# Sums of raw blocks of x by accumulating transfers instead of VectorE additions, in the weight gradient of a strided convolution

## The chip, the cores and the metric

The kernel runs on one core of a Trainium2 chip. TensorE multiplies matrices into PSUM, VectorE and ScalarE work element by element, and transfers run on 16 DMA engines that all queues share. A transfer is issued either by SP (SyncE) or by GpSimd (POOL in the profile); the profile shows the two as a hardware queue and a software queue. The metric is the time of one execution on the device in microseconds.

## The reference

A one-dimensional convolution with stride 2 (31 taps, 256 channels to 256), a normalization over time and a GELU, and then the gradients of all of it for a given `grad_out`:

```python
B, T, D, K = 2, 16000, 256, 31
s = 2
L = (T - K) // s + 1
h = jnp.einsum('blc,cd->bld', x[:, 0:s * L:s, :], w[0])
for i in range(1, K):
    h = h + jnp.einsum('blc,cd->bld', x[:, i:i + s * L:s, :], w[i])
mu = jnp.einsum('bld->bd', h)[:, None, :] / L
var = jnp.einsum('bld->bd', (h - mu) ** 2)[:, None, :] / L
h = (h - mu) / jnp.sqrt(var + 1e-5)
h = h * gn_gamma[None, None, :] + gn_beta[None, None, :]
return _gelu(h)
...
_out, _vjp = jax.vjp(_f, x, w, gn_gamma, gn_beta)
_grads = _vjp(grad_out)
```

The outputs are the forward result and the gradients for x, w, gamma and beta, in bfloat16. The change is in the gradient for w: for each tap i it is the sum over time of x at the tap's position times the gradient d of the convolution's output.

## The kernel before

The program has three large stages on TensorE: the forward convolution (with the GELU beside it), the gradient for x, and the gradient for w. The last one is the function `gradw` (line 1102) and the only one that the change touches.

**The algorithm of the stage.** The taps are split by the bits of their index, and each of three levels trades four products for three: two "corner" products, A and C, and a middle product B of the sum of two blocks of x with the difference of two blocks of d. Two levels give the nine combinations `COMBOS` (line 1100), n = 0 to 8; the third level is inside a combination. In combination n, x is needed as two tiles per half of the batch, `tgt[n, b, k3]` for k3 = 0 and 1, and as their sum `xs[n, b]`. A tile holds 128 partitions x 8 x 512 bf16 elements, 1 MB. Where neither outer level is a middle, a tile is one raw block of x, as `x_raws` lists it; with one middle it is the sum of two raw blocks, and in combination 3, which is (B, B), of four. These sums are the subject of the change.

**TensorE.** In each combination `leaf` runs 64 matmuls on the sums `xs` against d (two halves h, each over both b), then 64 on the tiles with k3 = 1 and 64 on those with k3 = 0, all 128x128 by 128x512. Four PSUM tiles hold the partial products; between them ScalarE copies and VectorE additions (`wps`, `p`, `we` in the profile) combine the three levels. `emit` makes a finished pair of taps in a tile `we`, of which there are two, and GpSimd stores it to `out_2`.

**VectorE.** Besides that it makes the differences of d (`d_sub` on the tiles D, E, S; `mk_dl` for the third level), the sums of raw blocks (`x_add`, 128x4096 elements) and the sums of the two tiles (`x_sum`).

**Transfers.** SP loads raw blocks with `raw` (line 1112: a tile's row is eight pieces of 1 KB from DRAM) and blocks of d with `d_raw` (the tiles D, E, S, 1216 KB). GpSimd stores `we`, and in the last two combinations also the late rows of `out_0`, which SP turns from `yd` into free x tiles (`out0_row`).

**Order.** It is written out by hand. Every engine works through its own queue in program order, and the program order follows a clock that counts TensorE's time: `advance(us)` moves it, `at(t, fn)` puts a step at a time, and `d_plan` and `x_plan` set the times of loads, additions and sums for combination n + 1 relative to the start T of combination n (a combination is some 41 us). So the times in the plans decide where an instruction stands in its engine's queue; when it then runs follows from the semaphores.

**Tiles.** `free` is a list of seven x tiles, and three more (`xe`) come from before the stage. A tile goes back with `release` when its matmuls are issued; the next write to it waits for TensorE to have read it: the tiles with k3 = 1 come free two thirds of the way through a combination, those with k3 = 0 at its end. Two fp32 tiles, `p2`, are lent to the list as `spare` in one combination. The tiles of combination 1, each a sum of two blocks, are kept as the first terms of combination 3 (`release` with n == 1).

**Before the change** `x_load(n, b, k3, j)` loads raw block j of a tile into a tile from `free`: j = 0 into the target itself, j > 0 into a temporary tile `tmp`. `x_add(n, b, k3, j)` with j > 0 adds the temporary tile to the target on VectorE and gives it back to `free`. With j = 0 it adds the tile of combination 0 to the raw block of combination 1, as (A, B) needs.

Of the kernel before, what the change touches and what calls it, by code (L numbers as in the profile page):

```python
# [12 lines left out]
ALU = mybir.AluOpType  # L13
# [17 lines left out]
def conv_stem_kernel(  # L31
# [14 lines left out]
    NB, T, C = x.shape  # L46
# [82 lines left out]
    te, ve, ac, gq, sp_ = (Engine(e) for e in (nc.tensor, nc.vector, nc.scalar, nc.gpsimd, nc.sync))  # L129
# [84 lines left out]
    def add2(out, a, b):  # L214
        return ve.tensor_tensor(out=out, in0=a, in1=b, op=ALU.add)
# [464 lines left out]
    def at(t, fn):  # L680
        clock[1] += 1
        events.append((t, clock[1], fn))
# [402 lines left out]
    def xblk(b):  # L1085
        t0 = 0 if b == 0 else NB * T - P * P
        return xf[t0:t0 + P * P, :].rearrange("(p f r par) c -> p f r (par c)", p=P, f=8, r=8, par=2)
# [14 lines left out]
    def gradw(px, po, psw, Dt, Et, St, x0):  # L1102
# [3 lines left out]
        xs_0 = [side["e"].tile([P, 2 * EH * 4], BF16, name="xh", tag="he", bufs=2)[:, 0:2048].rearrange("p (f n) -> p f n", f=4)  # L1106
                for _ in range(2)]
        free = [px.tile([P, 8, 512], BF16, name="x2", tag="x2", bufs=7)[:] for _ in range(7)]
# [3 lines left out]
        def raw(t, b, k3, k1, k2):  # L1112
            sp_.dma_start(out=t, in_=xblk(b)[:, :, 4 * k3 + 2 * k2 + k1, :])
            return t

        tgt, tmp = {}, {}

        def x_raws(n):
            i1, i2 = COMBOS[n]
            if (i1, i2) == (B_, B_):  # L1120
                return [None, (0, 1), (0, 0)]
            if (i1, i2) == (A, B_):
                return [(1, 0)]
            return [(k1, k2) for k1 in raws[i1] for k2 in raws[i2]]

        def x_load(n, b, k3, j=0):
            k = x_raws(n)[j]
            t = raw(free.pop(0), b, k3, *k)
            if j:
                tmp[n, b, k3, j] = t  # L1130
            else:
                tgt[n, b, k3] = t

        def x_add(n, b, k3, j):
            t = tgt[n, b, k3]
            if j:
                r = tmp.pop((n, b, k3, j))
                add2(t, t, r)
                free.append(r)
            else:  # L1140
                r = tgt[n - 1, b, k3]
                if r is xs_0:
                    for i in range(2):
                        add2(t[:, 4 * i:4 * i + 4], r[i], t[:, 4 * i:4 * i + 4])
                else:
                    add2(t, r, t)

        def x_sum(n, b):
            xs[n, b] = free.pop(0)
            if tgt[n, b, 0] is xs_0:  # L1150
                for i in range(2):
                    f = slice(4 * i, 4 * i + 4)
                    add2(xs[n, b][:, f], xs_0[i], tgt[n, b, 1][:, f])
            else:
                add2(xs[n, b], tgt[n, b, 0], tgt[n, b, 1])
# [49 lines left out]
        def x_plan(n, T):  # L1205
            def ld(t, n, b, k3, j=0):
                at(T + t, lambda: x_load(n, b, k3, j))

            def ad(t, n, b, k3, j):
                at(T + t, lambda: x_add(n, b, k3, j))  # L1210
            four = ((0, 1), (0, 0), (1, 1), (1, 0))
            if n == 1:
                for j, k in enumerate(four):
                    ld(1 + j, n, *k)
                    ad(18 + 4.2 * j, n, *k, 0)
            elif n in (2, 7, 8):
                for j, k in enumerate(four):
                    ld(1 + j, n, *k)
                if n == 2:
                    for j in (1, 2):  # L1220
                        ld(14 + j, 3, 0, 1, j)
                        ad(28 + j, 3, 0, 1, j)
            elif n == 3:
                for j, (t0, t1, b, k3, i) in enumerate(((14.5, 23, 0, 0, 1), (15, 25, 0, 0, 2), (15.5, 27.5, 1, 1, 1), (16, 29, 1, 1, 2),
                                                        (24, 34.5, 1, 0, 1), (26, 37, 1, 0, 2))):
                    ld(t0, n, b, k3, i)
                    ad(t1, n, b, k3, i)
            else:
                for k, t0, t1 in zip(four, (1, 3, 17.5, 20), (14.5, 17, 29.5, 32)):
                    ld(t0, n, *k)  # L1230
                    ld(t0 + 1, n, *k, 1)
                    ad(t1, n, *k, 1)
            for b in range(NB):
                at(T + ((36, 38.5) if n == 1 else (33.5, 38))[b], lambda b=b: x_sum(n, b))

# [95 lines left out]
        for n in range(9):  # L1331
            i1, i2 = COMBOS[n]
            T, d2, dl = clock[0], Et if i2 == B_ else Dt, {}
# [5 lines left out]
            if n == 7:  # L1339
                for i in range(8):  # L1340
                    t = T + (17 if i == 0 else 20.5 + 6 * i)
                    at(t, lambda i=i: out0_row(i, False))
                    at(t + 13, lambda i=i: out0_row(i, True))
            if n < 8:
                d_plan(n + 1, T)
                x_plan(n + 1, T)
# [17 lines left out]
            for i3, G in ((A, Y), (C_, X)):  # L1364
                k3 = 1 if i3 == A else 0
# [8 lines left out]
            if n == 2:  # L1374
# [10 lines left out]
                n=(14, 28, 42, 58, 82, 102, 150, 180, 228, 241, 262, 275, 298, 310, 332, 344),  # L1385
# [38 lines left out]
    def conv(b, c, ahead, prev):  # L1424
        nonlocal kn
        k, kn = kn, None

        def nxt():
            nonlocal kn
            if kn is None:  # L1430
                kn = FChunk(*ahead, xts.pop(ahead))
            return kn
        if ahead:
            at(clock[0] + 2, lambda: xts.__setitem__(ahead, fwd_load(*ahead)))
        return k, fwd_chunk_fixed(k, nxt if ahead else None, prev, advance)

    for c in range(1, NCK):
        k, prev = conv(0, c, (0, c + 1) if c + 1 < NCK else (1, 0), prev)
# [23 lines left out]
    for c in range(NCK):  # L1462
        k, prev = conv(1, c, (1, c + 1) if c + 1 < NCK else None, prev)
# [124 lines left out]
    for n, (b, c) in enumerate(seq):  # L1588
        k = kn
# [36 lines left out]
    with tc.tile_pool(name="px", bufs=1, reuse_waits="tile") as px, \  # L1626
            tc.tile_pool(name="psw", bufs=2, space=bass.MemoryType.PSUM, reuse_waits="tile") as psw:
        gradw(px, px, psw, Dt, Et, St[0], x0)
# [38 lines left out]
```

## Time and profile before

| | us |
|---|---|
| median of three runs (1272.4 to 1275.49) | 1272.7 |
| profiled execution | 1270.96 |
| span of its profile, first to last instruction | 1269.1 |
| first matmul of `gradw`, from the span's start | 893.0 |
| starts of combinations 1 to 8 | 935.3, 976.8, 1018.2, 1059.6, 1101.1, 1142.7, 1184.4, 1225.9 |
| VectorE addition of two 1 MB tiles | 2.28 |
| load of a block of x on SP's queue, median to landing | 8.6 |

The nine combinations can be told in the trace by the tiles that TensorE reads: `wps<-D,x` or `wps<-E,x` starts one, `wps<-dl,x` are its inner tiles. Nearly every instruction carries line 125, that of the recording helper, so groups are told apart by tile names. In the lines of the DMA queues q1 is SP's hardware queue and q0 GpSimd's software queue: packets, MB, and the time of their packets as a share of the 16 engines' span of the window. The DMA share in a window is the mean busy share of those engines. In the timeline, a bracket at the end of a line holds the idle time of the engine just before and what ended it.

### The profile page before, as it was taken

To read this page: it belongs to the slowest core of one execution; us is meant where nothing else is said; L and a number is where in the kernel's file an instruction comes from. 1 tells how busy PE (TensorE), PEld (TensorE's weight loads), DVE (VectorE), ACT (ScalarE), POOL (GpSimd) and SP (SyncE) were. 2 spreads that over 40 slices of the span, in tenths; PEclk is the share of its full clock that TensorE was granted. 3 is DMA by queue.
4 is the path that set the end of the run, shared out by engine and by line. 5 is a ranking of instruction groups with operands and counts; after the bars stand their busy time and mean duration, and the time that the engine had idled before them with its cause. 6 is when DMAs were issued, how large, how long until landed. Compare 5 with 4: busy or idle time off the path is not lost.

```text
span 1269.1 us, 19006 instructions
## 1 busy us (share of the span) xinstructions
PE 1233.0 (97%) x7692; PEld 758.6 (60%) x7692; DVE 901.7 (71%) x1080; ACT 504.0 (40%) x679; POOL 279.8 (22%) x410
## 2 busy tenths in 40 slices
PE   4899999999999999999999999999999999999998
PEld 2788889988888964444445444445444444444444
DVE  3967656578988687989876596685576755876482
ACT  0032423489888568989853333222011010101000
POOL 2013201112222433445333331100000000110043
PEclk9999999999999999999999999999999999999999
DMA  9979987439997796998649995455894795997895
GB/s 199 176 153 196 215 150 138 79 77 197 185 164 159 208 305 157 208 226 234 172 148 107 241 237 121 127 183 170 277 325 150 232 333 188 322 337 262 252 226 127
DMA packets 289335, 252.73 MB, mean 199 GB/s; under 512 B 197128, under 2 KB 260616, under 8 KB 284128
## 3 DMA queue, kind: packets, MB, share of 16 engines
q1 hardware_dynamic: 254448, 152.60, 50.7%
q0 software_dynamic: 30576, 96.82, 29.7%
q10 hardware_dynamic: 4224, 2.10, 0.8%
q8 instruction: 60, 0.98, 0.3%
q14 instruction: 27, 0.22, 0.1%
HBM read 136.42 MB, written 68.63 MB: 162 GB/s over the span
## 4 chain that ended last, share of the span: by engine, by line
PE 49%; DVE 3%; issue 2%; DMA 1%; ACT 1%; POOL 1%; POOLq 0%; DVEq 0%; ACTq 0%
PE wps L125 28%; PE ps L125 20%; DVE D L125 1%; DMA dyd<-gg 1%; DMA x<-in_x_dram 1%; DVE ps L125 0%; DVE et L125 0%; DVE le L125 0%; DVE go L125 0%; DVE ux L125 0%; POOL he L125 0%; DVE s L125 0%; DMA gg<-got 0%; DVE vk L125 0%; ACT gy L125 0%
## 5 line engine op out<-in xcount | busy, mean ns | idle before, releaser
L125 PEld LDWEIGHTS <-w 128*128 128x128 bf16 x3360 | 327.5, 98 | 57.7 <-issue 10.5
L125 PE MATMUL ps<-v,le 128*128 128x512 bf16 (+3 forms) x1152 | 259.2, 375 | 2.6 <-DVE ps L125 2.4
L125 PEld LDWEIGHTS <-le 128*128 128x128 bf16 (+1 forms) x1280 | 129.9, 102 | 144.8 <-issue 4.3
L125 PEld LDWEIGHTS <-x 128*128 128x128 bf16 x1248 | 122.0, 98 | 144.6 <-DVE x L125 0.6
L125 PE MATMUL ps<-la,w 128*128 128x256 bf16 (+2 forms) x1200 | 135.2, 273 | 18.0 <-DVE la L125 17.7
L125 PE MATMUL wps<-dl,x 128*128 128x512 bf16 (+1 forms) x704 | 150.8, 374 | 0.0
L125 ACT ACTIVATE ps<-ps 128x1024 f32<-128x1024 f32 (+3 forms) x115 | 85.2, 741 | 147.0 <-PE ps L125 147.0
L125 PE MATMUL ps<-lc,w 128*128 128x256 bf16 (+2 forms) x1168 | 129.2, 270 | 0.0
L125 ACT COPY p<-wps 128x1024 f32<-128x1024 f32 x28 | 28.4, 1013 | 211.2 <-PE wps L125 106.7
L125 DVE TENSOR_TENSOR go<-ps,rg 128x1024 bf16<-128x1024 f32 (+1 forms) x64 | 78.0, 1220 | 43.8 <-PE ps L125 29.1
L125 POOL DMA_DIRECT2D out_dram<-we x31 | 22.5, 726 | 334.6 <-DVE we L125 334.6
L125 PE MATMUL ps<-v,ux 128*128 128x512 bf16 (+1 forms) x384 | 90.7, 379 | 3.6 <-DVE ux L125 1.9
L125 PE MATMUL wps<-dl,xe 128*128 128x512 bf16 x416 | 91.7, 379 | 0.0
L125 PE MATMUL ps<-lx,w 128*128 128x256 bf16 (+2 forms) x768 | 86.9, 270 | 1.8 <-ACT ps L125 1.3
L125 ACT ACTIVATE gy<-gh,stats 128x1024 bf16<-128x1024 bf16 x64 | 76.6, 1228 | 7.3 <-DMA gh<-hd 7.3
L125 PE MATMUL wps<-D,x 128*128 128x512 bf16 x352 | 77.1, 379 | 0.0
L125 PEld LDWEIGHTS <-xe 128*128 128x128 bf16 x416 | 40.7, 98 | 49.1
L125 PEld LDWEIGHTS <-ux 128*128 128x128 bf16 (+1 forms) x384 | 38.7, 101 | 49.3 <-DVE ux L125 3.6
L125 ACT ACTIVATE hs<-ps 128x512 bf16<-128x512 f32 (+1 forms) x64 | 36.7, 578 | 75.9 <-PE ps L125 75.9
L125 DVE TENSOR_TENSOR ps<-ps,rb 128x1024 f32<-128x1024 f32 (+1 forms) x37 | 38.0, 1028 | 36.2 <-ACT rb L125 28.3
L125 ACT COPY rg<-ps 128x1024 f32<-128x1024 f32 (+1 forms) x32 | 32.2, 1007 | 69.2 <-PE ps L125 67.4
L125 DVE SCALAR_TENSOR_TENSOR gz<-gy,gy 128x1024 bf16<-128x1024 bf16 x32 | 39.1, 1222 | 23.9 <-ACT gy L125 22.8
(170 smaller groups left out, 1708.4 us busy)
## 6 DMA issues: line engine op xcount, KB each, us to landing
x<-in_x_dram SPq DMA_DIRECT2D x29, 1024.0 KB, 8.6
xe<-in_x_dram SPq DMA_DIRECT2D x20, 1024.0 KB, 9.2
S<-dnd SPq DMA_DIRECT2D x16, 1216.0 KB, 8.3
D<-dnd SPq DMA_DIRECT2D x12, 1216.0 KB, 9.2
out_dram<-go POOLq DMA_DIRECT2D x28, 512.0 KB, 4.2
gh<-hd POOLq DMA_DIRECT2D x32, 256.0 KB, 7.3
dnd<-dn POOLq DMA_DIRECT2D x32, 256.0 KB, 4.4
E<-dnd SPq DMA_DIRECT2D x6, 1216.0 KB, 10.6
```

Of the source, the lines that this page charges most:

```text
L125: ins = fn(*a, **k)
```

## The change

Where a tile is the sum of several raw blocks, the second and further blocks are no longer loaded into temporary tiles by SP and added by VectorE. Instead GpSimd issues a transfer with `accum_op=ALU.add` from x in DRAM into the target tile: the transfer adds the block to what the tile holds. This concerns 20 blocks: eight in combination 3 (two into each of its four tiles, on top of the tile kept from combination 1), and four each in combinations 4, 5 and 6. The temporary tiles are gone, and so the tiles go round in another order. The plan's times are new: in combinations 4 to 6 the plain loads stand at 1, 3, 13 and 15 us and the accumulating transfers at 9, 12, 22 and 25 (before: loads at 1, 2, 3, 4, 17.5, 18.5, 20 and 21, additions at 14.5, 17, 29.5 and 32); in combination 3's plan the six accumulating transfers stand at 2, 8, 12, 17, 21 and 26, and the two of its first tile at 29 and 37 in the combination before. An accumulating transfer waits for whatever wrote the tile before it. The function `add2` and all of the rest are unchanged.

```diff
         def x_load(n, b, k3, j=0):
-            k = x_raws(n)[j]
-            t = raw(free.pop(0), b, k3, *k)
+            k1, k2 = x_raws(n)[j]
             if j:
-                tmp[n, b, k3, j] = t
+                gq.dma_start(out=tgt[n, b, k3], in_=xblk(b)[:, :, 4 * k3 + 2 * k2 + k1, :], accum_op=ALU.add)
             else:
-                tgt[n, b, k3] = t
-
-        def x_add(n, b, k3, j):
-            t = tgt[n, b, k3]
-            if j:
-                r = tmp.pop((n, b, k3, j))
-                add2(t, t, r)
-                free.append(r)
+                tgt[n, b, k3] = raw(free.pop(0), b, k3, k1, k2)
+
+        def x_add(n, b, k3):
+            t, r = tgt[n, b, k3], tgt[n - 1, b, k3]
+            if r is xs_0:
+                for i in range(2):
+                    add2(t[:, 4 * i:4 * i + 4], r[i], t[:, 4 * i:4 * i + 4])
             else:
...
+                add2(t, r, t)
...
                 if n == 2:
                     for j in (1, 2):
-                        ld(14 + j, 3, 0, 1, j)
-                        ad(28 + j, 3, 0, 1, j)
+                        ld(21 + 8 * j, 3, 0, 1, j)
             elif n == 3:
-                for j, (t0, t1, b, k3, i) in enumerate(((14.5, 23, 0, 0, 1), (15, 25, 0, 0, 2), (15.5, 27.5, 1, 1, 1), (16, 29, 1, 1, 2),
-                                                        (24, 34.5, 1, 0, 1), (26, 37, 1, 0, 2))):
-                    ld(t0, n, b, k3, i)
-                    ad(t1, n, b, k3, i)
+                for t, b, k3, i in ((2, 0, 0, 1), (8, 1, 1, 1), (12, 0, 0, 2), (17, 1, 0, 1), (21, 1, 1, 2), (26, 1, 0, 2)):
+                    ld(t, n, b, k3, i)
             else:
-                for k, t0, t1 in zip(four, (1, 3, 17.5, 20), (14.5, 17, 29.5, 32)):
+                for k, t0, t1 in zip(four, (1, 3, 13, 15), (9, 12, 22, 25)):
                     ld(t0, n, *k)
-                    ld(t0 + 1, n, *k, 1)
-                    ad(t1, n, *k, 1)
+                    ld(t1, n, *k, 1)
```

More of the change, by code (lines that the diff above doesn't have):

```diff
@@ L1114, in raw @@
             return t
-        tgt, tmp = {}, {}
+        tgt = {}
         def x_raws(n):
@@ L1126, in x_load @@
         def x_load(n, b, k3, j=0):
-            k = x_raws(n)[j]
-            t = raw(free.pop(0), b, k3, *k)
+            k1, k2 = x_raws(n)[j]
             if j:
-                tmp[n, b, k3, j] = t
+                gq.dma_start(out=tgt[n, b, k3], in_=xblk(b)[:, :, 4 * k3 + 2 * k2 + k1, :], accum_op=ALU.add)
             else:
-                tgt[n, b, k3] = t
-        def x_add(n, b, k3, j):
-            t = tgt[n, b, k3]
-            if j:
-                r = tmp.pop((n, b, k3, j))
-                add2(t, t, r)
-                free.append(r)
-            else:
[L1141 to L1146, printed above, removed]
+                tgt[n, b, k3] = raw(free.pop(0), b, k3, k1, k2)
[4 more added lines that the diff above has]
+                    add2(t[:, 4 * i:4 * i + 4], r[i], t[:, 4 * i:4 * i + 4])
+            else:
+                add2(t, r, t)
         def x_sum(n, b):
@@ L1207, in ld, with ad @@
                 at(T + t, lambda: x_load(n, b, k3, j))
-            def ad(t, n, b, k3, j):
-                at(T + t, lambda: x_add(n, b, k3, j))
+            def ad(t, n, b, k3):
+                at(T + t, lambda: x_add(n, b, k3))
             four = ((0, 1), (0, 0), (1, 1), (1, 0))
@@ L1214, in x_plan @@
                     ld(1 + j, n, *k)
-                    ad(18 + 4.2 * j, n, *k, 0)
+                    ad(18 + 4.2 * j, n, *k)
             elif n in (2, 7, 8):
```

## The prediction

> **What bounds the kernel now.** I read the busy shares first, then the windows cut at the nine combinations of the weight gradient (the only code that the change touches), then the chain that ended last, and at the end the DMA queues in those windows, because the change turns VectorE work into transfers. From the page:
>
> ```profile
> PE 1233.0 (97%) x7692; PEld 758.6 (60%) x7692; DVE 901.7 (71%) x1080; ACT 504.0 (40%) x679; POOL 279.8 (22%) x410
> ```
>
> The windows of combinations 2 to 6 (us; then busy us of PE, PEld, DVE, ACT, POOL with counts; granted clock, DMA share, GB/s):
>
> ```profile
> 976.80:1018.20 41.40, 41.40 (x194) 18.74 (x192) 31.62 (x20) 4.06 (x4) 0.00 (x0) 1.00 0.62 189
> 1018.20:1059.60 41.40, 41.40 (x193) 18.81 (x192) 24.00 (x12) 6.05 (x6) 0.00 (x0) 1.00 0.88 289
> 1059.60:1101.10 41.50, 41.50 (x194) 18.80 (x193) 29.23 (x17) 4.05 (x4) 4.40 (x6) 1.00 0.82 268
> 1101.10:1142.70 41.60, 41.60 (x194) 18.80 (x193) 29.43 (x20) 4.05 (x4) 5.18 (x8) 1.00 0.97 339
> 1142.70:1184.40 41.70, 41.55 (x192) 18.69 (x192) 27.58 (x15) 6.05 (x6) 2.06 (x3) 1.00 0.81 278
> ```
>
> TensorE fills every combination: 192 matmuls of 0.216 us are 41.4 us, which is the window. VectorE is busy for 24 to 32 us of it, so taking VectorE work away frees nothing. The DMA engines are the second resource, at 0.97 in combination 5. The chain shows that this is already the tight place:
>
> ```profile
> 1099.95 39.30 PE wps L125 x182
> 1139.24 0.02 issue
> 1139.26 7.14 DMA x<-in_x_dram
> 1146.40 0.02 issue
> 1146.42 53.70 PE wps L125 x248
> ```
>
> Between 1139 and 1146 the chain runs through a load of x, and the timeline shows what that costs TensorE (idle 0.26 and 0.64 us):
>
> ```profile
> 1142.66 3.12 PEld L125 LDWEIGHTS <-x 128*128 128x128 bf16 x15 [0.26 <-issue]
> 1146.41 3.57 PEld L125 LDWEIGHTS <-x 128*128 128x128 bf16 x18 [0.64 <-DVE x L125]
> ```
>
> These 0.9 us are the whole idle time of TensorE in the stage, and so the most the change can win.
>
> **The change part by part.** *Removed from VectorE:* 20 additions of 128x4096 at 2.28 us, 45.6 us. Cover: TensorE's 41.4 us per combination. Worth 0, at most the 0.9 us above.
>
> *Removed from SP:* the 20 loads of 1 MB that fed them. What stays on SP moves up past them, but most of it waits for TensorE to release a tile (SP waited 110 us in the stage for that), so it starts little earlier. Worth 0.
>
> *Issue on GpSimd:* 20 issues. A store of hs has as many pieces (1024) and took 0.89 to 0.92 us, so 18 us over four combinations on an engine busy for 5 us of 41 there. Worth 0.
>
> *New waits on GpSimd's queue:* an accumulating transfer waits until the plain load of its tile has landed, and the second one into a tile of combination 3 waits for the first. Behind it in the queue stand the stores of we (combinations 4 and 5); two we tiles rotate, so a late store holds VectorE's next we addition, and that holds the PSUM tile that TensorE needs. In combinations 2 and 3 nothing stands behind. I cost it at nothing by itself: two of a combination's four accumulations stand ahead of its first store, and the other two wait for loads that have landed some 17 to 28 us into it (three blocks and two D in a row are 16.4 us of the engines, more with accumulations between), while the second group of stores leaves 29 us into combination 4 today (1089.0).
>
> *The last stores of out_0:* the tiles that the late transposes take change. Two of the four are now free only when combination 8 starts (1225.9), where today their transposes start at 1221.6. Their stores leave at 1256.6, 13 us after the last transpose was issued, so a shift of 4 us is hidden.
>
> *The transfers themselves* decide. The trace has no accumulating transfer; its nearest rows on the page (KB each, median us from issue to landing) are
>
> ```profile
> x<-in_x_dram SPq DMA_DIRECT2D x29, 1024.0 KB, 8.6
> ...
> out_dram<-go POOLq DMA_DIRECT2D x28, 512.0 KB, 4.2
> ```
>
> Call a the time that one 1 MB block takes of all 16 DMA engines. A plain load of a block, from combination 2, where the queue moved almost nothing else:
>
> ```profile
> q1 hardware_dynamic: 7720, 7.79, 61.6%
> ```
>
> 61.6% of 41.4 us is 25.5 us for 7.79 MB, so 3.43 us a block (1.05 MB). Lower bound: a = 3.43, if reading the old content of the tile hides behind the read of x. A read of SBUF is priced by the stores of we in combination 5:
>
> ```profile
> q0 software_dynamic: 384, 1.05, 6.5%
> ```
>
> 1.05 MB cost 6.5% of 41.6 us, 2.70 us. If an engine does both reads one after the other, a = 3.43 + 2.70 = 6.13. Upper bound, nothing overlapped: the landing time of a load (8.6 us) and of two 512 KB stores (4.2 each), a = 17. I take 6.13: it lies nearest to the rows that count engine time and not latency, and many pieces are in flight in every transfer here. A rule speaks against the change at this very place. The Trainium skill, Collectives: The Full Stack, section "The bandwidth ceiling: the fold count and why AG ≠ RS ≠ AR", says that a reducing transfer puts two reads per piece on one read ring, and gives 62.28 against 32.35 GB/s, a ratio of 1.93. By it a would be 6.6 (an estimate: 1.93 times 3.43) and the end some 9 us later than mine; no run here shows it.
>
> Now the demand on the DMA engines by combination, with 3.43 for a block of x, 3.07 for a load of D, E or S (combination 1: 30.7 us for 11.24 MB, of which 3.77 MB of x took 12.3; six loads remain), 2.7 for eight stores of we:
> - combination 2: 6 accumulations, half of one left over from combination 1, 2 loads of E: 6.1 + 6.5a
> - combination 3: 4 blocks, 2 D, 4 accumulations: 19.9 + 4a
> - combination 4: the same and the stores: 22.6 + 4a
> - combination 5: 4 blocks, 4 loads of E and S, stores, 4 accumulations: 28.7 + 4a
>
> Together 77.3 + 18.5a against 4 x 41.4 = 165.8 us of TensorE. At a = 3.43 combination 5 needs 42.4, which is what it does today (8 loads instead of 4 and 4). At a = 6.13 the four need 45.9, 44.4, 47.1 and 53.2, together 190.7: 24.9 us too much. No combination shows a share over 0.97, so 190.7 becomes 196.6: 5.9 more. At three of the ends (of 2, 4 and 5) TensorE then stands until the last accumulation has landed and VectorE has made the sum: 2.3 (shortest landing 5.7 less 3.43) + 2.28, less the 3.45 us of 16 matmuls that run before the second half's sum is needed, 1.1 each, 3.3 in all. At the last of them a load of the next combination stands in the other queue and takes 3.4 of the engines' time. Sum: 24.9 + 5.9 + 3.3 + 3.4 - 0.9 (today's idle time) = +36.6 us. The profiled execution took 1270.96 us (span 1269.1), so 1307.6; the median of the runs shown is 1.7 above it: 1309 us.
>
> **The rivals.** *The second read is hidden (not slower).* For it: reads and writes of an engine may overlap, and in combinations 2 and 3 the share is 0.62 and 0.88, so there is room. Against: in combination 5 there is none. It decides at one point: with a up to 4.4, combination 5 needs 46.3, 4 us more than today, combination 4 40.2, and the end moves by less than 0.3% (about what a measurement of this kernel can tell from no change). Time 1271.8 (a = 3.43 and no idle time) to 1276.5. A gain over 0.3% would need 3.8 us of idle time where the trace has 0.9; I leave it a rest for what I have overlooked in the stage before.
>
> *The pieces are handled one after another (much slower).* If an engine waits for one sum before the next read, a goes by latency; the nearest row is a load's landing, 8.6 us. Then 77.3 + 159.1 = 236.4, 70.6 too much, 7.3 for the share, 6.7 for the ends, -0.9: +83.7, so 1356 and more. Against it: a load of 1 MB lands after 8.6 us though each engine has 64 pieces of it, so pieces of plain transfers do overlap.
>
> *The stores behind the accumulations become the wait.* If a plain load lands late, GpSimd's queue stands and with it the stores of we. VectorE's third we addition of combinations 4 and 5 would then be late by up to one accumulation, some 6 us: 12 us on top of the forecast, 1321. It needs the transfers to be late first, so it is a part of the slower cases.
>
> That the change does not do what it says is excluded: the program as built has 20 additions fewer on VectorE, 20 loads fewer on SP and 20 transfers more on GpSimd.
>
> **How the numbers follow.** Forecast, a from 4.4 to 8.6: chance 0.52 (with the stores' rival 0.07 of it), own range 1277 to 1356, likeliest 1309. Hidden: 0.26, of which 0.03 for faster by over 0.3% and 0.23 within it. One after another: 0.22. So faster 0.03, within 0.3% 0.23, slower 0.74. The range goes from 1268, which takes in the hidden case, to 1362, which takes in the beginning of the last one; some 0.18 lies above.
>
> **What would show it.** Right: accumulating transfers with a DMA share near 1 in combinations 2 to 5, TensorE idle at the starts of combinations 3, 5 and 6 behind an addition of x (the sum) that waits for a transfer of GpSimd's queue, combinations 0, 1, 7 and 8 unchanged at 41.4. GpSimd's queue time for 20 MB of accumulations gives a directly: 123 us of 16 engines at 6.13. Wrong: a DMA share in combination 5 that stays at 0.97 with TensorE full (hidden), or landings of tens of us while the share is low (latency, not engine time). A loss outside combinations 2 to 6 would mean that I have missed a place.

## The result and the profile after

| | before | after |
|---|---|---|
| median, us | 1272.88 (1272.4 to 1275.49) | 1296.99 (1295.31 to 1297.97) |
| profiled execution, us | 1270.96 | 1297.31 |
| stage: first matmul of `gradw` to the start of combination 8, us | 893.01 to 1225.86: 332.85 | 894.11 to 1252.25: 358.14 |

The change makes the kernel slower: ratio 1.0183, 95% interval 1.0167 to 1.0199, some 24.1 us. The forecast was 1309, 36.6 us more than before. The stage alone grew by 25.3 us; combinations 0, 1, 7 and 8 did not grow. Further down I compare stages too, because the time at which the stage begins differs by some us from one profiled execution to the next (889 to 906 in the runs of this study), although everything ahead of it is the same program.

The line of busy times of the page of after, and its software queue, which now carries the 20 blocks:

```profile
PE 1236.8 (95%) x7692; PEld 759.3 (59%) x7692; DVE 857.1 (66%) x1060; ACT 503.8 (39%) x679; POOL 309.6 (24%) x430
...
q0 software_dynamic: 51376, 117.80, 39.3%
```

VectorE has lost its 20 additions (901.7 to 857.1 us, 1080 to 1060 instructions), GpSimd has 20 instructions more and is busy for 29.8 us more. TensorE has the same 7692 matmuls but is busy for 3.8 us more: some matmuls run slower.

The windows of combinations 2 to 6 of after (us; busy us of PE, PEld, DVE, ACT, POOL with counts; granted clock, DMA share, GB/s):

```profile
977.90:1019.30 41.40, 41.40 (x194) 18.77 (x193) 13.30 (x10) 4.05 (x4) 7.29 (x6) 1.00 1.19 207
1019.30:1062.70 43.40, 41.57 (x193) 18.67 (x192) 14.86 (x8) 6.04 (x6) 6.08 (x5) 1.00 1.13 267
1062.70:1104.20 41.50, 41.50 (x194) 18.84 (x193) 23.25 (x15) 4.05 (x4) 8.84 (x9) 1.00 1.05 255
1104.20:1162.20 58.00, 44.38 (x194) 19.40 (x193) 24.27 (x16) 4.05 (x4) 11.82 (x12) 0.85 0.98 247
1162.20:1210.80 48.60, 43.44 (x193) 19.11 (x192) 26.21 (x14) 6.05 (x6) 1.42 (x2) 0.93 0.76 253
```

Combination 3 is 2 us longer than before, 5 is 16.4, 6 is 6.9; 2 and 4 are as long as ever. The DMA share is above 1 in combinations 2 to 4 and 0.98 in 5, while the GB/s are lower than before in 3 to 6: in 3, 4 and 5 the engines are busier than before and move less. (Packet times overlap, so a share can pass 1.) The granted clock falls to 0.85 and 0.93 in the two long ones. The timeline of TensorE in after shows the three places (start, busy us; in brackets the idle time just before and what ended it):

```profile
1024.74 10.53 PE L125 MATMUL wps<-E,x 128*128 128x512 bf16 x48 [1.83 <-DVE x L125]
...
1121.41 13.28 PE L125 MATMUL wps<-D,x 128*128 128x512 bf16 x48 [13.62 <-DVE x L125]
...
1170.93 12.42 PE L125 MATMUL wps<-E,x 128*128 128x512 bf16 x48 [5.17 <-DVE x L125]
```

Each stands 16 matmuls into a combination, where the sum for the second half of the batch is needed. The idle times are 20.6 us together. The same 48 matmuls took 10.53 us after 1.8 us of idle time, but 13.28 and 12.42 after the long ones: 4.6 us more. 20.6 + 4.6 is 25.2, next to a growth of 25.3 us; some tenths of idle time, which the kernel before has as well, make up the rest. The waits of after in the stage (us in total, times, longest) give what stands behind it:

```profile
DVE x L125 <- DMA x<-in_x_dram: 40.3, 2, 20.4
DVE x L125 <- DMA xe<-in_x_dram: 35.6, 3, 14.8
...
PE wps L125 <- DVE x L125: 20.6, 3, 13.6
```

TensorE waits for VectorE's sum, and VectorE for an accumulating transfer.

**The price of a block.** Between 977.9 and 1002 GpSimd's queue moved accumulations and nothing else ran; the DMA view of after there:

```profile
DMA packets 4501, 4.56 MB, mean 189 GB/s; under 512 B 64, under 2 KB 4500, under 8 KB 4500
...
q0 software_dynamic: 4500, 4.54, 120.4%
```

From 988 on it runs at 193 to 195 GB/s, so a block of 1.05 MB takes 5.4 us of the 16 engines, against 3.43 for a plain load: 1.57 times. (The 5.4 goes by the clock and the 3.43 by the time of the packets. By the clock, the plain loads of before move 301 GB/s from 990 to 1009, at a share of 0.97: 3.5 us a block, nearly the same.) It can be added to plain loads: from 1005 to 1018, 1.57 MB of accumulations (1.5 blocks, 8.1 us) and 1.55 MB of SP's loads (1.48 blocks, 5.1 us) filled 13 us.

**The place in the queue.** The chain of waits of after, from 1083 to 1171, goes through both long stops:

```profile
1083.66 1.24 DVE we L125
...
1086.66 0.22 POOL x L125
...
1087.59 31.39 DMA x<-in_x_dram
...
1119.07 2.30 DVE x L125
...
1121.41 20.20 PE wps L125 x80
...
1145.54 22.60 DMA xe<-in_x_dram
...
1168.58 2.30 DVE x L125
```

An accumulating transfer starts only when GpSimd has stored a `we`, and then the transfers take 31.4 and 22.6 us. GpSimd's timeline shows why it starts there:

```profile
1085.19 1.48 POOL L125 DMA_DIRECT2D out_dram<-we  x2 [18.24 <-DVE we L125]
1086.66 3.02 POOL L125 DMA_DIRECT2D x<-in_x_dram  x2
...
1123.01 1.42 POOL L125 DMA_DIRECT2D out_dram<-we  x2 [22.59 <-DVE we L125]
1124.42 1.52 POOL L125 DMA_DIRECT2D x<-in_x_dram  x1
...
1143.15 1.48 POOL L125 DMA_DIRECT2D out_dram<-we  x2 [15.71 <-DVE we L125]
1144.63 3.00 POOL L125 DMA_DIRECT2D xe<-in_x_dram  x2
```

In the plans of combinations 5 and 6 the second pair of accumulations (22 and 25 us) stands behind the first stores of `we`, and those wait for VectorE's `we`, which waits for TensorE. GpSimd stood for 18 and 16 us with accumulations behind. How much of that is delay follows from when the plain loads of the same tiles had landed. For combination 5 these loads were issued at 1059.5 and 1074.0 and landed after 14.2 and 10.7 us, so the place in the queue held up the first accumulation of the pair by 13 us and the second by only 3. For combination 6 it held up both by 20 us or more.

The stop at combination 5 also passed some of its delay on to combination 6. It held up the store at 1123.01, whose `we` needs TensorE, and behind that store stood the first pair of combination 6: its plain loads had landed 29 and 20 us before the accumulations were issued.

**Packets in turn.** The DMA views of after show how two blocks then take 31 us. In the first 4.4 us GpSimd's queue moved 19 packets; at combination 6 it was the same, 23 packets in 4.5 us, and no run shows why. From 1092 to 1104, beside SP's loads of x in pieces of 1 KB, it moved 1.39 MB, and both queues got as many packets (465 and 464 from 1096 to 1100). Then SP's queue loads E and S; from 1104 to 1108:

```profile
q1 hardware_dynamic: 160, 1.32, 81.3%
q0 software_dynamic: 156, 0.16, 24.6%
```

Again the two queues got as many packets, 160 and 156. But a packet of SP was 8.3 KB, and one of the accumulation 1 KB: 0.16 MB in 4 us, a fifth of the 0.78 that the queue moves alone. From 1104 to 1116 it moved 0.56 MB in all, beside SP's 3.69. The Trainium skill, DMA: Bandwidth & Descriptors, section "Queues, rings and completion order", says that an engine takes the queues in turn and switches at packets; the trace agrees, 160 to 156, and adds the price: who has the small packets gets the small share.

### The profile page after: what moved, and what is told of

Its sections match the earlier page's. It is cut to its first block, busy times and chain, and to the rows that moved or that the text cites. A ratio compares the mean times of both kernels' runs of the same rounds, so it can differ in the third digit from the quotient of the medians.

```text
span 1295.5 us, 18994 instructions
## 1 busy us (share of the span) xinstructions
PE 1236.8 (95%) x7692; PEld 759.3 (59%) x7692; DVE 857.1 (66%) x1060; ACT 503.8 (39%) x679; POOL 309.6 (24%) x430
## 4 chain that ended last, share of the span: by engine, by line
PE 56%; DMA 12%; DVE 11%; issue 10%; ACT 8%; POOL 1%; SPq 1%; DVEq 0%; POOLq 0%; ACTq 0%
PE ps L125 42%; PE wps L125 15%; DMA x<-in_x_dram 6%; ACT gy L125 3%; DVE gy L125 2%; DVE ps L125 2%; DMA xe<-in_x_dram 2%; ACT gs L125 2%; DVE gz L125 2%; DMA hd<-hs 1%; DMA he<-hd 1%; SPq L125 1%; DVE s L125 1%; ACT hs L125 1%; ACT ps L125 1%
## 5 line engine op out<-in xcount | busy, mean ns | idle before, releaser
L125 PEld LDWEIGHTS <-x 128*128 128x128 bf16 x1184 | 116.7, 99 | 164.6 <-DVE x L125 22.1
L125 PE MATMUL wps<-dl,x 128*128 128x512 bf16 x640 | 140.1, 379 | 0.0
L125 PE MATMUL wps<-dl,xe 128*128 128x512 bf16 (+1 forms) x480 | 101.8, 372 | 0.0
L125 PE MATMUL wps<-D,x 128*128 128x512 bf16 x352 | 80.0, 388 | 13.6 <-DVE x L125 13.6
L125 PEld LDWEIGHTS <-xe 128*128 128x128 bf16 x480 | 47.0, 98 | 53.4
L125 POOL DMA_DIRECT2D out_dram<-go x32 | 23.4, 733 | 140.0 <-DVE go L125 128.2
## 6 DMA issues: line engine op xcount, KB each, us to landing
x<-in_x_dram POOLq DMA_DIRECT2D x14, 1024.0 KB, 16.4
```

Of the source, the lines that this page charges most:

```text
L125: ins = fn(*a, **k)
```

## The experiments

Twelve kernels were run. The expectations count the theories so: the first, the engines' time for accumulations; the second, the place in GpSimd's queue; the third, that a software queue is slow as such. A fourth, packets in turn, came up with the 4 KB version. Each ratio is to executions of before that ran together with the kernel; their medians lie between 1269.6 and 1272.9 us. "Stage" is the growth of the stage in the profiled execution, "idle" TensorE's idle times in it with their combination.

| kernel | median us | ratio to before, 95% | stage | idle (combination) |
|---|---|---|---|---|
| after | 1296.99 | 1.0183 (1.0167 to 1.0199) | +25.3 | 1.83 (3), 13.62 (5), 5.17 (6) |
| plain transfers | 1269.1 | 0.9973 (0.9955 to 0.9991) | -0.5 | none |
| second pair early | 1284.16 | 1.0103 (1.005 to 1.0156) | +10.7 | 1.17 (3), 7.41 (5) |
| combination 3 alone | 1272.07 | 1.001 (0.9987 to 1.0034) | +1.2 | 1.53 (3) |
| 4 to 6 alone | 1298.53 | 1.0205 (1.0166 to 1.0244) | +30.1 | 3.78 (4), 14.03 (5), 4.98 (6) |
| early, loads first | 1285.17 | 1.012 (1.0077 to 1.0163) | +14.9 | 1.47 (3), 11.16 (6) |
| 4 KB pieces | 1278.87 | 1.0067 (1.0041 to 1.0093) | +9.6 | 7.84 (6) |
| early, without 6 | 1271.25 | 0.9997 (0.9966 to 1.0029) | +5.9 | 3.30 (3) |
| 4 KB version, 1 KB pieces | 1297.0 | 1.0223 (1.0191 to 1.0255) | +25.3 | 1.09 (3), 13.63 (5), 6.03 (6) |
| 4 KB pieces, early | 1276.63 | 1.0048 (1.0016 to 1.008) | -0.5 | none |
| combination 6 alone, early | 1283.14 | 1.0101 (1.0074 to 1.0128) | +10.3 | 8.66 (6) |
| D, E, S in small pieces | 1288.66 | 1.0141 (1.0101 to 1.0181) | +16.3 | 6.29 (5), 6.02 (6) |
| the same, early | 1280.85 | 1.0075 (1.005 to 1.0099) | +12.0 | 0.35 (4), 1.58 (5), 8.09 (6) |

### Plain transfers in the same places

```diff
-                gq.dma_start(out=tgt[n, b, k3], in_=xblk(b)[:, :, 4 * k3 + 2 * k2 + k1, :], accum_op=ALU.add)
+                gq.dma_start(out=tgt[n, b, k3], in_=xblk(b)[:, :, 4 * k3 + 2 * k2 + k1, :])
```

> The 20 transfers of GpSimd stay where they are, with the same waits, but overwrite the tile and do not add (the sums of raw blocks are left out, so the gradient of w is that of single blocks). Theory 1, the accumulating transfer takes too much of the DMA engines (5.4 us a block read off the rate of 195 GB/s while GpSimd's queue runs alone, against 3.43 for a plain load): the loss goes, 1271 to 1276 us, and GpSimd's queue alone moves 300 GB/s or more. Theory 2, the place in GpSimd's queue (the second pair of combinations 4 and 5 waits behind the first store of we): the place is unchanged, so most of the 24 us stays, over 1288. Theory 3, transfers of the software queue are slow as such: 195 GB/s again and over 1288.

No loss; TensorE has no idle time in the stage. GpSimd's queue is the same, the second pair stands behind the stores of `we` as in after:

```profile
1078.63 1.43 POOL L125 DMA_DIRECT2D out_dram<-we  x2 [28.92 <-DVE we L125]
1080.06 1.77 POOL L125 DMA_DIRECT2D x<-in_x_dram  x2
```

and the DMA view of the same kernel, from 977.9 to 1005, gives 3.23 us a block (52.0% of 27.1 us for 4.57 MB, 4.36 blocks):

```profile
q0 software_dynamic: 1196, 4.57, 52.0%
```

So neither the place nor the software queue costs anything as long as the transfers are plain; the time is even 2 us below the range that I had given for the first theory. The run changed more than I had meant, though: without the accumulation the queue made packets of 3.8 KB (4.57 MB in 1196), not of 1 KB. It tells accumulating transfers from plain ones, and not whether the engines' time or the size of the packets does it; the version with 4 KB pieces below tells these apart.

### The second pair ahead of the stores of we

```diff
-                for k, t0, t1 in zip(four, (1, 3, 13, 15), (9, 12, 22, 25)):
+                for k, t0, t1 in zip(four, (1, 3, 13, 15), (9, 12, 19, 20)):
```

> As the changed kernel, but the second pair of accumulating transfers of combinations 4 to 6 stands at 19 and 20 us of the plan, ahead of the first store of we in GpSimd's queue. Theory 1 (the engines' time alone: 77.3 + 18.5 x 5.4 = 177.2 us of demand against 165.8): the order does not change the demand, so 1290 to 1298 as now. Theory 2 (place in the queue): the pair starts when its plain loads have landed, some 5 us earlier in combination 4 and up to 20 us in combination 5, so the 13.6 and 5.2 us of idle time shrink to under half, 1275 to 1285.

The timeline of TensorE in this kernel has two stops left, and none at combination 6:

```profile
1035.66 10.53 PE L125 MATMUL wps<-E,x 128*128 128x512 bf16 x48 [1.17 <-DVE x L125]
...
1126.12 12.74 PE L125 MATMUL wps<-D,x 128*128 128x512 bf16 x48 [7.41 <-DVE x L125]
```

Two numbers of the plan take 14.6 us off the stage, and the time is in the range of the second theory, though the stop at combination 5 has not shrunk to under half, as that theory had it. What is left there is another wait: the second accumulation of the pair went out at 1101.38, when its plain load had landed, 15.9 us after that was issued. What stays of the stage's growth, 10.7, is near the 11.4 that the demand of my prediction gives with the measured price of a block (77.3 + 18.5 x 5.4 = 177.2 us against 165.8), but 2.2 us of it are slower matmuls.

### Which combinations lose

Accumulations in combination 3 alone (all else by VectorE, as before), and in 4 to 6 alone; the core of the first edit, to the kernel before (the second has `n != 3`):

```diff
+            if j and n == 3:
+                k1, k2 = k
+                gq.dma_start(out=tgt[n, b, k3], in_=xblk(b)[:, :, 4 * k3 + 2 * k2 + k1, :], accum_op=ALU.add)
+                return
```

> Only combination 3's eight blocks by accumulating transfers; combinations 4 to 6 as before, by VectorE. Theory 1: combination 2 needs 6.1 + 6.5 x 5.4 = 41.2 us of 41.4, so at most the 1.8 us of idle time that the changed kernel has there: 1272 to 1276. Theory 2 says the same here (no store of we stands in the queue by then). A cost that goes with the number of accumulating transfers wherever they stand would give 8/20 of the loss, 1282.

> The other part: twelve blocks of combinations 4 to 6 by accumulating transfers, combination 3's by VectorE. Theories 1 and 2: the whole loss but 2 us, 1292 to 1298, idle time of TensorE at the starts of combinations 5 and 6 and half clock after each idle time above 5 us. By the number of transfers: 12/20, 1287.

The eight blocks of combination 3 cost nothing that can be measured: they run in combination 2 and at the end of 1, and in combination 2 the DMA share was 0.62 before. The twelve others cost the whole, and a little more than I had expected: stops of 14.03 and 4.98 us at combinations 5 and 6, like those of after. The stop at combination 4 (3.78 us, and 2.78 for the slower matmuls) is not in after, and I hadn't foreseen it. The chain of waits of this kernel leads from it to a plain load on SP's queue that took 29.6 us beside accumulations. The accumulation into the same tile went out at 1045.55 and landed 46.3 us after the start of combination 3. In after it landed after 44.1 us, and combination 3 itself was 2 us longer, so nothing waited for it.

### Early, and the plain loads first

```diff
-                for k, t0, t1 in zip(four, (1, 3, 13, 15), (9, 12, 22, 25)):
+                for k, t0, t1 in zip(four, (1, 2, 3, 4), (9, 12, 19, 20)):
```

> As the run with the early second pair, and on SP the second pair of plain loads of combinations 4 to 6 stands ahead of the loads of D, E and S (plan times 1, 2, 3, 4). If the rest of the loss (1284 us, 10.7 us in the stage) is still a matter of order, because the second pair waits for plain loads that stand behind loads of D, it shrinks again, 1273 to 1279. If it is the engines' time, 177 us of demand against 165.8, the order can't help: 1280 to 1288, with the idle time only moved, to the start of combination 6, since D, E and S then come later.

With the plain loads ahead of those of D, E and S the stop at combination 5 is gone, and a longer one is at combination 6:

```profile
1158.07 12.90 PE L125 MATMUL wps<-E,x 128*128 128x512 bf16 x48 [11.16 <-DVE x L125]
```

The stop moved, and the stage lost 14.9 us instead of 10.7. Putting one transfer ahead of another did not help here, which fits engines that have too much to do in sum.

### Without combination 6, and combination 6 alone

Both with the early pair; the first accumulates in combinations 3, 4 and 5 (16 blocks), the second in 6 (four blocks, whose transfers run during combination 5; its condition is `n == 6`):

```diff
+            if j and n in (3, 4, 5):
```

> Sixteen blocks by accumulating transfers: combinations 3, 4 and 5, with the early second pair; combination 6's four as before, loaded by SP and added by VectorE. The engines' demand is then 41.2, 41.5 and 44.2 us in combinations 2 to 4 and 42.4 in combination 5, 169.3 against 165.8. Engines' time: a loss of some 4 to 6 us, 1275 to 1279. By the number of transfers: 16/20 of the 12.7 us of the early run, 1281 to 1282. If the place in combination 5 were of no account, no change from the early run, 1284.

> Only the four blocks of combination 6 come by accumulating transfers (second pair ahead of the first store of we); all other sums are made by VectorE as in the kernel before. These transfers run in combination 5. If the engines' time is what counts, this window alone needs 28.7 + 4 x 5.4 = 50.3 us in 41.6, while combination 4 ahead of it has 5 us to spare only as far as its loads can be early: 4 to 9 us of TensorE's idle time at the start of combination 6, with 2 more for the half clock after it, so 1276 to 1282 us (ratio 1.004 to 1.009), against none at all for the 16 other accumulations without these four. If the loss needs the backlog of all twenty, the time stays within 0.3% of the kernel before.

Sixteen blocks cost nothing that can be measured, less than I expected (the profiled execution with the stop of 3.30 us, 1275.66, was the slowest of ten, and the median is 1271.25), and the four of combination 6 alone cost 13.6 us, 10.3 of them in the stage (I had expected 1282 us at most). Combination 5, where they run, is the one in which the DMA share was 0.97 before. TensorE's one stop in the second kernel:

```profile
1157.87 12.45 PE L125 MATMUL wps<-E,x 128*128 128x512 bf16 x48 [8.66 <-DVE x L125]
```

The demand of that window with the measured price is 28.7 + 4 x 5.4 = 50.3 us, 8.8 more than the 41.5 there are; the stop is 8.66. That the two agree so closely is partly chance, since the slower matmuls add 1.9 us to the stop. For the sixteen, the demand of combinations 2 to 4 is 41.2 + 41.5 + 44.2 = 126.9 against 124.2: 2.7 too much, which room elsewhere may have taken; no run shows that.

### Larger pieces

The accumulating transfers read consecutive rows of x, in pieces of 4 KB; what they add is then not what the sums need.

```diff
-                gq.dma_start(out=tgt[n, b, k3], in_=xblk(b)[:, :, 4 * k3 + 2 * k2 + k1, :], accum_op=ALU.add)
+                gq.dma_start(out=tgt[n, b, k3], in_=x.rearrange("b t c -> (b t) c")[0:16 * P, :].rearrange("(p f r) c -> p f (r c)", p=P, f=8, r=2), accum_op=ALU.add, max_dma_last_dim=4096)
```

> As the changed kernel, but each accumulating transfer takes its 1 MB from consecutive rows of x, in 256 pieces of 4 KB in place of 1024 of 1 KB (the gradient of w then sums other blocks). Asks what sets the 5.4 us of a block. If it is a cost per byte read (source and old content, 195 GB/s whatever the pieces), the rate of GpSimd's queue alone stays at 190 to 200 GB/s and the time at 1292 to 1298. If a large part is a cost per piece, as loads of D with 9.7 KB rows move 400 GB/s against 306 for x, the rate rises to 215 to 260 GB/s, a block takes 4 to 4.9 us and the time falls to 1278 to 1290.

The answer was split, as no theory had it. GpSimd's queue alone, from 982 to 1000, moved 207 GB/s, only 6% more than in after (5.06 us a block). The plain transfers of the same queue, in packets of 3.8 KB, moved 305 GB/s from 980 to 990 in their kernel. So most of the price comes from the adding and not from small pieces; but the loss of the stage fell from 25.3 to 9.6 us. The DMA view of this kernel with both queues at work, from 1144 to 1148, shows what else is different:

```profile
q0 software_dynamic: 183, 0.69, 86.5%
q1 hardware_dynamic: 187, 0.19, 17.0%
```

Again as many packets on both sides, but now the accumulation has the larger ones and gets 0.69 MB of 0.88. To tell the size of the pieces from the other addresses, the same rows in 1 KB pieces:

```diff
- ... max_dma_last_dim=4096)
+ ... max_dma_last_dim=1024)
```

> As the version with accumulating transfers from consecutive rows of x, but cut into pieces of 1 KB again (1024 pieces a block, as in the changed kernel); what is added to the tiles are other rows of x than the sums need. If the size of the pieces gave that version its smaller loss, GpSimd's queue alone goes back to 193 to 198 GB/s, and the time to 1292 to 1299 us (ratio 1.016 to 1.021). If it was the addresses (whole stretches of x in place of every sixteenth row), the rate stays at 205 to 210 GB/s and the time at 1276 to 1282 us.

The stage loses 25.3 us again, as in after, with stops like those of after (13.63 us at combination 5 and 6.03 at 6), and GpSimd's queue alone moves 194 GB/s (992 to 1012). It was the size of the pieces. And the 4 KB version with the early pair:

> As the version with 4 KB pieces, and the second pair of accumulating transfers of combinations 4 to 6 stands ahead of the first store of we. With 5.05 us a block the sum of the demand of combinations 2 to 5 is 77.3 + 18.5 x 5.05 = 170.7 us, 4.9 more than TensorE needs. If the loss is this excess, and the rest of what the 4 KB version loses (9.6 us in the stage) comes from the order, as in the changed kernel, the stage grows by 4 to 6 us: 1274 to 1278 us (ratio 1.003 to 1.006), with idle time of TensorE at one combination's start only. If the order matters no longer at this rate, 1277 to 1281 as before.

Its time is in the expected 1274 to 1278, but not for the expected reason: its profiled execution (1277.81) has no stop at all in the stage (332.4 us), where I had 4 to 6 us of excess. The 6.8 us that it took more than the profiled execution of before lie ahead of the stage (it begins at 899.8, before at 893.0), in the part that is the same in both. So the demand sum is good to some 5 us and no better.

### Loads of D, E and S in small pieces

If packets go in turn, the accumulations should win where SP's packets become small, although the engines then have more to do.

```diff
-                at(T + t, lambda: d_raw(tile, b, k, j0))
+                at(T + t, lambda: d_raw(tile, b, k, j0, max_dma_last_dim=1216))
```

(`d_raw` hands the limit on to its transfer; those lines are left out here.)

> As the changed kernel, but the loads of D, E and S in the stage are cut into pieces of 1.2 KB (1024 pieces of 1216 bytes instead of some 8 KB each). If the engines give the two queues packets in turn (in the changed kernel 156 accumulating packets moved beside 160 of SP's between 1104 and 1108, but 0.16 MB beside 1.32), the accumulations get 0.4 to 0.5 MB in 4 us beside such a load instead of 0.16, the sum for the second half of combination 5 lands 5 to 10 us earlier, and TensorE's 13.6 us there shrink to 4 to 9. Smaller pieces cost the engines more (D, E and S then at a block's 3.3 to 4.1 us instead of 3.07), some 6 us over combinations 2 to 5, so the whole comes to 1283 to 1293 us (ratio 1.009 to 1.016). If only the engines' time per byte counts, the smaller pieces add their cost: 1299 to 1306 us.

> The same with the second pair of accumulating transfers of combinations 4 to 6 ahead of the first store of we. If order and packets in turn are two separate causes, this comes out below both: 1276 to 1284 us (ratio 1.004 to 1.01), the rest being the engines' time (11 us too much in combinations 2 to 5, and the cost of the smaller pieces). If the early order has already taken away what the large packets cost, it is no faster than the early order alone: 1284 to 1290 us.

The DMA view of the first kernel, from 1100 to 1104, beside a load of E:

```profile
q0 software_dynamic: 447, 0.46, 70.5%
q1 hardware_dynamic: 446, 0.53, 45.3%
```

0.46 MB in 4 us instead of 0.16, and the stop at combination 5 is 6.29 us instead of 13.62:

```profile
1109.81 13.06 PE L125 MATMUL wps<-D,x 128*128 128x512 bf16 x48 [6.29 <-DVE x L125]
...
1159.97 11.88 PE L125 MATMUL wps<-E,x 128*128 128x512 bf16 x48 [6.02 <-DVE x L125]
```

So the large packets of E and S held up the accumulation, as the fourth theory says; with them gone the stage loses 16.3 us, 9.0 less. With the early pair as well it is 12.0. Its time, 1280.85, lies in the range that I had given for two separate causes, but the ratios of the two early kernels (1.0103 and 1.0075) can't be told apart by their intervals, and the stage speaks against it: small pieces take 9.0 us off, the early pair 14.6, both together 13.3. The two causes don't add. They look like two ways out of one delay, the late second pair beside large packets. What neither takes away, 11 to 12 us, is near what the engines have too much to do in sum, 11.4; that it is this, I argue from the sum and have not shown.

None of the kernels that compute the sums is faster than the kernel before; with combination 3 alone, or without combination 6, it is as fast.

## Why the prediction was right, and where it was not

The kernel became slower for the reason that I had named first: accumulations cost the DMA engines more than plain loads, and combinations 2 to 5 have no room for it. That 1297 is near 1309 is partly luck. The price of a block was too high by enough to make 13.5 us of excess, 12.6 us of smaller terms were not seen, and 14.6 us of the measured 25.3 go with an order that I had costed at nothing.

**TensorE fills the stage, and what VectorE and SP lose is worth 0.** Held. In the version with plain transfers, which also lacks the 20 additions and SP's 20 loads, the stage is 0.5 us shorter; the most I had allowed was 0.9. (Its median is 2.3 us below that of before; 1.8 of that lie outside the stage or between executions.) Those 0.9 us I had read from the lines of the weight loads (PEld). The matmuls themselves lost half of that: combinations 5 and 6 of before last 41.58 and 41.75 us, against 41.44 for an undisturbed one.

**Issue on GpSimd.** 0.9 us each was too low: 1.49 us (median of 14), against 0.88 for the plain ones. Worth 0 all the same.

**The price of a block, a = 6.13.** It held that an accumulation costs the engines more and that combinations 2 to 5 have no room for it; the size was off. It measured 5.4, 1.97 us more than a plain load where I had added 2.70. That the difference is a second read, partly hidden, fits, but no run shows it. The sign that I had named, the time of GpSimd's queue, would have misled: by the time of its packets a block takes 6.7 us (120.4% of 24.1 us for 4.54 MB), because packets overlap. The rule that I had weighed (the Trainium skill, Collectives: The Full Stack, "The bandwidth ceiling: the fold count and why AG ≠ RS ≠ AR") with its 1.93 is further off; here the ratio is 1.57 at most. With 5.4 the excess of the demand is 11.4 us and not 24.9. That is the term that made the forecast too high: 24.9 + 5.9 + 3.3 + 3.4 - 0.9 becomes some 22.7.

**The terms for the share, the ends and the neighbour (12.6 us).** Not seen. With the second pair early the stage grows by 10.7, and with small pieces as well by 12.0, about the bare excess of 11.4; the window of combination 5 alone gives a stop of 8.66 for 8.8. But with the loads first it is 14.9 for the same sum, so terms of a few us can't be excluded. That my sum with 5.4 comes to 22.7 and the stage grew by 25.3 is a coincidence of terms that I could not find with causes that I had not priced.

**The order on GpSimd's queue, costed at nothing.** This is the step that failed. I asked what stands behind the accumulations (the stores of `we`), and not behind what the accumulations stand. They stood behind the stores; putting them ahead takes 14.6 us off the stage. I had written that "the other two wait for loads that have landed some 17 to 28 us into it"; in fact GpSimd waited for `we`, 18.2 and 15.7 us, and three of the four accumulations were ready 13 us or more before they went out. It also turned the places round: I expected stops at combinations 3, 5 and 6, which came, but not that the one at 5 would be the longest by far. My rival "the stores behind the accumulations" had the queue the wrong way round.

**Packets in turn, not in the prediction.** I took the engines' time as one pot. How the two queues share it decides who is late, and the 1 KB packets of the accumulation lost against 8.3 KB: with SP's packets made small the stage is 9.0 us shorter, with the order as it is.

**The slower matmuls, not in the prediction.** 4.6 us. Where TensorE stood for up to 1.83 us the next 48 matmuls took 10.53 us; after 3.30 us and more, in all the kernels here, 11.88 to 13.50. Single matmuls then take 0.427 instead of 0.216 us. The Trainium skill, TensorE: Matmul & The Clock Gate, says in "HAM oscillation — how this bites in real kernels" that a long enough wait for transfers throttles TensorE again to half its clock, and in "Part 1: The HAM clock gate" that the way up takes some 3.4 us; the trace agrees on the halving (0.427 us a matmul; the granted clock of 0.85 is the mean of a window in which it was halved for a part), and on the time it has 1.4 to 3.0 us lost, that is 2.7 to 5.9 us at half speed, on both sides of that figure.

**The last stores of `out_0`.** Held: combinations 7 and 8 are as long as before.

**The rivals.** "The second read is hidden" needed a price up to 4.4, "one after another" 8.6; at 5.4 neither is the case.

What stays open: what makes up the price of an accumulation; why GpSimd's queue moves hardly a packet in the first 4.4 us after the late issues; and why the 4 KB version with the early pair has no stop, though its demand is some 5 us too much.

## What to carry to other kernels

Moving an addition off an engine that is not the bottleneck and into the transfers pays for it with DMA time (here some 1.5 times a plain load), so count the DMA time of every window before, not only the engine that is relieved: the same change was free in windows at a share of 0.62 to 0.88 and cost 13.6 us with four blocks where it was 0.97. For a moved step ask both ways on its new queue, what waits behind it and what it waits behind; a store that follows the slowest engine is a bad thing to stand behind. Where two queues share the engines, compare their packet sizes: with 1 KB against 8 KB a transfer gets a ninth of the bytes.

## What the runs showed of the hardware

- An accumulating transfer into SBUF: 193 to 195 GB/s with 1 KB packets and 207 with 4 KB, alone on the 16 engines; plain loads, by the time of their packets, 306 (3.43 us a block, 1 KB packets) and 324 (3.23, 3.8 KB), and by the clock 301 and 305 in the windows above.
- Its issue on GpSimd: 1.49 us for 1024 pieces, 1.21 for 256 pieces of 4 KB; the plain one of the same block, which leaves in packets of 3.8 KB, 0.88.
- While both queues had work they got equal numbers of packets, whatever their size: 465 to 464, 156 to 160, 183 to 187, 447 to 446.
- TensorE's matmuls ran at half speed after an idle time of 3.3 us or more, and not after 1.83 or less; each time 1.4 to 3.0 us were lost.
